# A long convolution and a gated layer on one core: the first batch's last step cut in four parts, some of its matrices made earlier, and work shared out anew in the first steps

## The chip, the cores and the metric

The kernel runs on one core of a Trainium2 chip. A core has five engines that run side by side, each working through its own queue in order: TensorE (PE in the profile; PEld is its weight load), VectorE (DVE), ScalarE (ACT), GpSimd (POOL) and SyncE (SP), which here issues all DMA transfers. They meet through semaphores. The metric is the time of one execution on the device in microseconds (us); of several runs the median counts.

## What is computed

```python
def _attn_ref(x, v, pos_emb, w1, w2):           # x, v: (4, 12480, 128)
    h_mlp = np.maximum(pos_emb @ w1, 0.0) @ w2
    window = np.exp(-0.01 * pos)[:, None]
    h_filt = h_mlp * window                      # a filter as long as the sequence
    u = x * v
    y = irfft(rfft(u, n=2 * S) * rfft(h_filt, n=2 * S))[:, :S, :]
    return x * y                                 # -> 49920 rows of 128

def _moe_ref(x, w_in, w_out):                    # w_in: 128 x 2048, w_out: 2048 x 128
    h = x @ w_in
    g = h * np.cos(h)
    return g @ w_out
```

All is float32; the weights of the gated layer arrive as 64-bit numbers and are converted on the chip.

## The kernel before

**The convolution.** The transform of each batch is written as matrix products over a sequence cut into 120 x 96 places. A batch goes through: the product u = x * v with sums and differences of mirrored rows (30 units, `u_units`, lines 381 to 391); a first forward step (`f1_units`, 64 units: PE L394, then the result is evicted from PSUM, in `f1_evict`, by ACT for even units and by DVE for odd ones, `f1_takers`); a second forward step, which also multiplies with the transformed filter (`f2_units`, 48 units); a first inverse step (`i1_units`, 64 units: PE L457, ACT copies half of the result to `other` at L465, DVE adds and subtracts it at L467), called the third step here; and the last step (`i2_units`, 30 units of four rows each: PE L482 with four matrices `tm`, DVE multiplies by x at L487, SP stores to `zd`). The filter goes through the first two steps as well, before and beside batch 0.

**The matrices of the last step.** A matrix is rows of sines and cosines turned by an angle (`turn`, L271 to L287): ACT multiplies one table (L280), and then DVE multiplies the other and adds in one instruction (L282); or, where a `spare` buffer is given, POOL multiplies (L285) and adds (L287). For batch 0 each unit of `i2_units` makes its four matrices in `before`, three with DVE and one with POOL, all at once and one unit ahead, and SP stores the group to `td`; batches 1 to 3 load their groups from `td`.

**The tables.** `Tables.sines` computes the arguments of a sine table in four or five instructions on one engine (DVE for the forward tables, POOL for the inverse ones) and then has ACT take the sine (L219). The inverse tables are made beside the filter's first step: one sine for each five parts of the step.

**The conversions.** `convert_units` turns the 64-bit weights to float32 in eight pieces, w_in beside batch 0's first step and w_out beside its third, one piece in fourteen parts of the step. A piece has `float32_parts` (DVE two instructions, POOL three, ACT two) and `float32_join` (DVE L151, POOL L156; for w_in a store to memory). The join of a piece stands behind the parts of the next.

**The order of the work.** It is written out by hand: each of these is a generator, and `units` yields after each part with what that part is worth in gate steps. Before batch 0's last step there is no gated layer yet, and the stages follow each other. From then on the main loop walks 98 row tiles x 16 gate steps (`moe_up`, L691 to L700; `moe_act`, L705 and L707; `moe_down`, L716), and after each step takes parts of the convolutions until the step's worth is used up. One unit of batch 0's last step is worth `FIRST_STEPS` = 3.4 gate steps. `inverse_units` takes parts of the next batch's product beside it. The first gate tile can start when two groups of batch 0 have come back from `zd`.

Of the kernel before, what the change touches and what calls it, by code (L numbers as in the profile page):

```python
# [30 lines left out]
def kernel(  # L31
# [135 lines left out]
    def convert_units(pool, pieces):  # L167

        raws, half = [], None
        for i in range(len(pieces) + 1):  # L170
            while len(raws) < min(i + 2, len(pieces)):
                raws.append(pool.tile([P, WCOL, 2], U32, name="raw", bufs=3))
                nc.sync.dma_start(raws[-1][:, :, :], pieces[len(raws) - 1][1])
            yield
            last = half
            if i < len(pieces):
                half = float32_parts(pool, raws[i])
            if i > 0:
                float32_join(pieces[i - 1][0], raws[i - 1], *last)


    class Tables:
        def __init__(self, pool, engine):
            self.pool, self.engine = pool, engine
            self.prod, self.moved = (
                pool.tile([P, P], F32, name=name) for name in ("prod", "moved"))
# [8 lines left out]
        def sines(self, row, column, turn, outs, eighths=None):  # L195


            p, n = outs[0][0].shape
            base = self.prod[0:p, 0:n]
            self.engine.tensor_scalar(out=base, in0=row[0:p, 0:n],  # L200
                                    scalar1=column[0:p, 0:1], scalar2=None, op0=ALU.mult)
            if eighths is not None:
                self.engine.tensor_scalar(out=base[:, eighths], in0=base[:, eighths],
                                        scalar1=float(turn // 8), scalar2=None, op0=ALU.add)
            for dst, quarters in outs:
                turned = self.pool.tile([P, P], F32, name="turned", bufs=2)
                m, t = self.moved[0:p, 0:n], turned[0:p, 0:n]
                if isinstance(quarters, int):
                    quarters = float(quarters * turn // 4)
                self.engine.tensor_scalar(out=m, in0=base, scalar1=quarters,  # L210
                                        scalar2=None, op0=ALU.add)

                self.engine.tensor_scalar(out=t, in0=m, scalar1=1.0 / turn, scalar2=ROUND,
                                        op0=ALU.mult, op1=ALU.add)
                self.engine.tensor_scalar(out=t, in0=t, scalar1=ROUND, scalar2=float(turn),
                                        op0=ALU.subtract, op1=ALU.mult)
                self.engine.tensor_tensor(t, m, t, op=ALU.subtract)
                yield
                nc.scalar.activation(dst, t, AF.Sin, scale=TWO_PI / turn)  # L219

    def forward_tables(pool):
        t = Tables(pool, nc.vector)
# [22 lines left out]
    def inverse_tables(pool):  # L245

        t = Tables(pool, nc.gpsimd)
# [12 lines left out]
                           eighths=slice(H - 1, N2, H))  # L260
        for kept, made in ((csd, cs), (rowsd, rows), (twd, tw_t)):
            nc.sync.dma_start(kept[:, :, :], made[:, :, :])
# [9 lines left out]
    def turn(dst, first, second, one, other, half=None, spare=None):  # L272


        term = dst
        if half is not None:
            term = half()[0:dst.shape[0], 0:math.prod(dst.shape[1:])]
            if len(dst.shape) == 3:
                term = term.rearrange("p (a b) -> p a b", a=dst.shape[1])
        nc.scalar.activation(term, first, AF.Copy, scale=one)  # L280
        if spare is None:
            nc.vector.scalar_tensor_tensor(out=dst, in0=second, scalar=other, in1=term,  # L282
                                           op0=ALU.mult, op1=ALU.add)
        else:
            nc.gpsimd.tensor_scalar(out=spare, in0=second, scalar1=other, scalar2=None,  # L285
                                    op0=ALU.mult)
            nc.gpsimd.tensor_tensor(dst, term, spare, op=ALU.add)  # L287
# [110 lines left out]
    def f1_takers(b):  # L398

        if b % 2 == 0:  # L400
            return nc.scalar.copy, lambda out, in_: nc.scalar.activation(
                out, in_, AF.Copy, scale=-1.0)
# [3 lines left out]
    def f1_evict(ps, b):  # L406
        copy, negated = f1_takers(b)
# [7 lines left out]
    def f1_evict_filter(ps, b):  # L415

        copy, negated = f1_takers(b)
# [82 lines left out]
    def units(n, steps, before, mm, after, parts, ahead=2):  # L500

        for j in range(min(ahead, n)):
            before(j)
        yield 0.0
        last = iter(())
        for j in range(n):
            if j + ahead < n:
                before(j + ahead)
            now = None
            for i in range(parts):  # L510
# [4 lines left out]
                next(last, None)  # L515
                yield steps / parts
            next(last, None)
# [4 lines left out]

    REST = 3.0
    U_STEPS, F1_STEPS, F2_STEPS, I1_STEPS, I2_STEPS = 2.0, 0.8, 2.9, 0.8, 1.5
    FIRST_STEPS, I2U_STEPS = 3.4, 3.0
# [21 lines left out]
    def f1_units(bank, u, evict=f1_evict):  # L547
# [6 lines left out]
        return units(CB, F1_STEPS, lambda j: None, mm, lambda j, ps: evict(ps, j), 2)  # L554
# [57 lines left out]

    def i2_units(bank, b, bufs):

        with tc.tile_pool(name="back", bufs=2) as pool:
            ts, xss = {}, {}

            def before(j):
                ts[j] = pool.tile([N1, G, 2, R], F32, name="tm", bufs=bufs)
                if b == 0:  # L620
                    for i in range(G):
                        if i < G - 1:
                            make_t(ts[j][:, i, :, :], n2s(j)[i])
                        else:
                            spare = pool.tile([N1, 2, R], F32, name="spare", bufs=1)
                            make_t(ts[j][:, i, :, :], n2s(j)[i], spare=spare[:, :, :])
                    nc.sync.dma_start(td[j, :, :, :, :], ts[j][:, :, :, :])
                else:
                    nc.sync.dma_start(ts[j][:, :, :, :], td[j, :, :, :, :])
                xss[j] = pool.tile([R, 2, UA * D], F32, name="xs", bufs=bufs)  # L630
                load_pairs(xss[j], x, b, n2s(j)[0], n2s(j)[UA])

            def mm(j, ps, i):
                if i == 0:
# [5 lines left out]
                             lambda j, ps: i2_out(pool, ps, xss.pop(j), b, j), 2,  # L640
                             ahead=bufs - 1)

    def inverse_units(bank, b):
# [3 lines left out]
        if b + 1 == B:  # L647
            yield from i2_units(bank, b, 3)
            return
        new = u_units(b + 1, 3, slots[0:R, :, :, :], lambda j, half: nc.vector,  # L650
                      side="right")
        for i, steps in enumerate(i2_units(bank, b, 2)):
            if i >= 5:
                for _ in range(1 + i % 2):
# [90 lines left out]
    with tc.manual_schedule():  # L745
        with tc.tile_pool(name="psum", bufs=8, space=PSUM) as psum, \
# [14 lines left out]
            with tc.tile_pool(name="layers", bufs=1, side="right") as pool:  # L761
# [8 lines left out]
                for i in range(1, NCH):  # L770
                    pes[i] = filter_load(pool, i)
                first_u = u_units(0, 3, slots[0:R, :, :, :],
                                  lambda j, half: nc.vector if half and j % 3 else nc.gpsimd)
# [29 lines left out]
            f1 = f1_units(bank, ftile[0:FR, :, :, :], f1_evict_filter)  # L803
# [13 lines left out]
            def beside(units, pieces, bufs):  # L817
                with tc.tile_pool(name="convert", bufs=bufs) as pool:
                    convert = convert_units(pool, pieces)
# [3 lines left out]
                    for _ in convert:  # L823
                        pass

            beside(f1_units(bank, slots[0:R, :, :, :]), [(wind[:, c], w) for c, w in in_pieces], 1)
# [16 lines left out]
            beside(i1_units(bank), [(w_out_sb[:, c, :], w) for c, w in out_pieces], 1)  # L843
# [83 lines left out]
```

## Time and profile before

| what | us |
|---|---|
| median of three runs (3817.17 to 3817.78) | 3817.72 |
| the profiled execution | 3821.13 |
| its span, first to last instruction | 3819.3 |
| PE busy in the span | 3713.3 (97%) |
| DVE busy | 2804.5 (73%) |
| ACT busy | 2488.4 (65%) |
| POOL busy | 2559.8 (67%) |

The profile is that of one execution. "Busy" adds up instructions; an idle engine is shown with what released it ("0.55 <-ACT other L465": idle 0.55 us until ACT's instruction that wrote `other`). A group row gives line, engine, operation, tiles and shapes, count, then busy us and mean ns of one, then idle time before it and its releasers. A row of a stretch gives the busy times of the engines between two points of the span, with the number of instructions in brackets. A line number is a line of the kernel before; helpers such as `turn` and `u_multiply` carry the line for all who call them.

### The profile page before, as it was taken

The page shows a single profiled execution, that of the slowest core. Times are in us where ns is not written, and L with a number is a line of the kernel's source. Part 1 is how long each engine was busy: PE and PEld are TensorE (multiplying, and loading weights), DVE is VectorE, ACT ScalarE, POOL GpSimd, SP SyncE. Part 2 cuts the span into 40 slices and gives each one's busy share as a digit, 9 for nine tenths or more (in the row PEclk, how much of TensorE's full clock was granted, in tenths as well). Part 3 has the DMA queues.
Part 4 walks back from the last instruction along what each step waited for, and adds up shares of the span by engine and source line. Part 5 has one row for each costly group of instructions (what it writes and reads, how often), then busy time and mean ns, then how long its engine had stood idle before and what let it go on. Part 6 is the DMA issues. An engine that isn't in the chain of part 4 may idle for free.

```text
span 3819.3 us, 47226 instructions
## 1 busy us (share of the span) xinstructions
PE 3713.3 (97%) x13546; PEld 2117.3 (55%) x13546; DVE 2804.5 (73%) x5737; ACT 2488.4 (65%) x4597; POOL 2559.8 (67%) x2307
## 2 busy tenths in 40 slices
PE   7797989999999999999999999999999999999999
PEld 6777545655566555545566556555566544444444
DVE  7796898678876787787766787787765566666666
ACT  5654666766665556766655567666664677777777
POOL 6564776478854665588845664788644577777776
PEclk9898999999999999999999999999999999999999
DMA  6163442022201651122203640222105200000000
GB/s 164 49 174 93 134 144 79 12 72 78 77 25 29 188 175 30 31 75 78 68 12 96 182 131 12 57 75 77 49 18 164 83 17 22 18 17 23 17 17 17
DMA packets 209082, 274.65 MB, mean 72 GB/s; under 512 B 17062, under 2 KB 146486, under 8 KB 208694
## 3 DMA queue, kind: packets, MB, share of 16 engines
q1 hardware_dynamic: 208822, 271.63, 24.5%
q8 instruction: 109, 1.79, 0.2%
q14 instruction: 151, 1.24, 0.1%
HBM read 191.93 MB, written 79.63 MB: 71 GB/s over the span
## 4 chain that ended last, share of the span: by engine, by line
PE 85%; DVE 5%; POOL 3%; DMA 3%; ACT 2%; issue 2%; SPq 0%; DVEq 0%; POOLq 0%; ACTq 0%
PE ph L691 32%; PE acc L716 28%; PE cv L716 5%; PE cv L482 5%; PE cv L457 4%; PE cv L394 3%; PE cv L433 3%; PE ph L126 2%; POOL f L700 2%; DMA hd<-h 2%; PE ps L457 1%; ACT cs L705 1%; DVE k L697 1%; PE ps L394 1%; DVE xt L382 1%
## 5 line engine op out<-in xcount | busy, mean ns | idle before, releaser
L700 POOL TENSOR_TENSOR f<-a,k 128x512 f32<-128x512 f32 x1568 | 1989.4, 1269 | 1070.6 <-DVE k L697 1067.8
L691 PE MATMUL ph<-at,w_in_sb 128*128 128x512 f32 x3136 | 1602.7, 592 | 18.6 <-DVE gt L707 18.2
L694 ACT ACTIVATE a<-ph,quarter 128x512 f32<-128x512 f32 x1568 | 1073.3, 684 | 756.9 <-PE ph L691 747.8
L716 PE MATMUL acc<-gt,w_out_sb 128*128 128x512 f32 x2656 | 1362.4, 594 | 5.5 <-ACT ot L722 5.3
L707 DVE TENSOR_TENSOR gt<-ph,cs 128x512 f32<-128x512 f32 x1568 | 1078.1, 688 | 326.4 <-ACT cs L705 298.2
L697 DVE TENSOR_SCALAR k<-a 128x512 f32<-128x512 f32 x1568 | 781.5, 498 | 599.4 <-ACT a L694 583.6
L705 ACT ACTIVATE cs<-f 128x512 f32<-128x512 f32 x1568 | 980.3, 625 | 363.8 <-POOL f L700 362.2
L716 PEld LDWEIGHTS acc<-gt,w_out_sb 128*128 128x128 f32 x2656 | 500.9, 189 | 651.2 <-issue 614.1
L691 PEld LDWEIGHTS ph<-at,w_in_sb 128*128 128x128 f32 x3136 | 553.9, 190 | 358.3 <-issue 262.9
L452 POOL TENSOR_TENSOR slots<-slots,t 120x256 f32<-120x256 f32 x384 | 310.9, 816 | 63.0 <-DVE t L451 25.8
L482 PEld LDWEIGHTS cv<-slots,tm 96*104 96x104 f32 x1920 | 243.0, 172 | 100.0 <-issue 86.0
L482 PE MATMUL cv<-slots,tm 96*104 96x128 f32 x1920 | 254.6, 275 | 3.8 <-DVE tm L282 3.8
L716 PE MATMUL cv<-gt,w_out_sb 128*128 128x512 f32 (+1 forms) x480 | 238.5, 579 | 1.0 <-DVE gt L707 1.0
L457 PEld LDWEIGHTS cv<-cs,slots 120*96 120x96 f32 x1536 | 176.9, 167 | 69.1 <-issue 68.7
L457 PE MATMUL cv<-cs,slots 120*96 120x120 f32 x1536 | 183.2, 266 | 0.0
L433 PE MATMUL cv<-slots,w 124*120 124x256 f32 x576 | 173.0, 380 | 0.0
L433 PEld LDWEIGHTS cv<-slots,w 124*120 124x120 f32 x576 | 103.3, 184 | 122.4 <-issue 109.4
L394 PEld LDWEIGHTS cv<-c,slots 104*124 104x124 f32 x768 | 132.8, 192 | 63.8 <-issue 58.3
L716 PEld LDWEIGHTS cv<-gt,w_out_sb 128*128 128x128 f32 x480 | 90.9, 190 | 110.2 <-issue 106.9
L394 PE MATMUL cv<-c,slots 104*124 104x192 f32 x768 | 150.4, 326 | 0.0
L382 DVE TENSOR_TENSOR xt<-xt,vt 104x256 f32<-104x256 f32 x200 | 143.0, 717 | 0.7 <-DMA vt<-in_v_dram 0.4
L467 DVE TENSOR_TENSOR slots<-cv,other 96x240 f32<-96x240 f32 x384 | 133.6, 394 | 2.8 <-ACT other L465 2.8
(125 smaller groups left out, 2529.3 us busy)
## 6 DMA issues: line engine op xcount, KB each, us to landing
h<-hd SPq DMA_DIRECT2D x144, 240.0 KB
tm<-td SPq DMA_DIRECT2D x90, 312.0 KB
xt<-in_x_dram SPq DMA_DIRECT2D x120, 208.0 KB
vt<-in_v_dram SPq DMA_DIRECT2D x120, 208.0 KB
xs<-in_x_dram SPq DMA_DIRECT2D x120, 208.0 KB
zd<-zs SPq DMA_DIRECT2D x120, 208.0 KB
zb<-zd SPq DMA_DIRECT2D x97, 256.0 KB
w<-wd SPq DMA_DIRECT2D x144, 116.2 KB
```

The lines of the kernel that those rows point to most:

```text
L394: nc.tensor.matmul(ps[0:KE, i * 2 * N1:(i + 1) * 2 * N1], u[:, b, 0:KE, i], c1[0:u.shape[0], :, :].rearrange("p r k -> p (r k)"), start=Tr ...
L433: nc.tensor.matmul(pi, w[:, i, :], parts[0:KE, :, k], start=True, stop=True)
L452: nc.gpsimd.tensor_tensor(y[:, r], y[:, r], t[:, r], op=op)
L457: nc.tensor.matmul(ps[0:N1, (i * 2 + r) * N2:(i * 2 + r + 1) * N2], parts[0:N2, r, :, b, i], cs[:, r, :], start=True, stop=True)
L482: nc.tensor.matmul(ps[0:R, i * D:(i + 1) * D], t[:, i, r, :], slots[0:N1, :, place, :], start=(r == 0), stop=(r == 1))
L691: nc.tensor.matmul(ph[:, 0:m], w_in_sb[:, c * P:(c + 1) * P], ats[n][:, 0:m], start=True, stop=True)
L694: nc.scalar.activation(a[:, 0:m], ph[:, 0:m], AF.Identity, bias=quarter[:, 0:1], scale=INV_TWO_PI)
L697: nc.vector.tensor_scalar(out=k[:, 0:m], in0=a[:, 0:m], scalar1=ROUND, scalar2=ROUND, op0=ALU.add, op1=ALU.subtract)
L700: nc.gpsimd.tensor_tensor(f[:, 0:m], a[:, 0:m], k[:, 0:m], op=ALU.subtract)
L705: nc.scalar.activation(cs[:, 0:m], f[:, 0:m], AF.Sin, scale=TWO_PI)
L707: nc.vector.tensor_tensor(gt[:, 0:m], ph[:, 0:m], cs[:, 0:m], op=ALU.mult)
L716: nc.tensor.matmul(accs[n][:, 0:m], w_out_sb[:, c, :], gt[:, 0:m], start=(c == 0), stop=(c == NFC - 1))
```

## The change

1. `turn`: where a `spare` is given, its multiply goes from POOL to ACT; POOL keeps the addition.
2. `make_group`: the four matrices of a group are made one at a time, with a yield after each. In batch 0's last step two of four go by DVE and two by ACT and POOL.
3. `SOME`: groups 4, 9, 14, 19, 24 and 29 are made beside batch 0's third step instead, all four matrices by ACT and POOL, and stored; batch 0 loads them like the other batches.
4. `units` takes a generator from `before` and advances it by one with each part; batch 0's last step has four parts a unit instead of two, and is worth 3.5 gate steps a unit.
5. Batch 1's product: in every second unit POOL multiplies the first half. Batch 0's product: from unit 18 on POOL multiplies both halves.
6. `f1_takers` gives ACT 53% of the filter's units (33 of 64) and 55% of batch 0's (35 of 64).
7. `Tables`: for the inverse tables the sine on ACT is issued one table later, with three buffers instead of two.
8. `convert_units`: the join of a piece stands ahead of the parts of the next.

```diff
@@ convert_units
-            last = half
+            if i > 0:
+                float32_join(pieces[i - 1][0], raws[i - 1], *half)
             if i < len(pieces):
                 half = float32_parts(pool, raws[i])
-            if i > 0:
-                float32_join(pieces[i - 1][0], raws[i - 1], *last)
@@ Tables.sines (lag 1 for the forward tables, 2 for the inverse ones)
-                turned = self.pool.tile([P, P], F32, name="turned", bufs=2)
+                turned = self.pool.tile([P, P], F32, name="turned", bufs=self.lag + 1)
...
+                self.waiting.append((dst, t, TWO_PI / turn))
                 yield
-                nc.scalar.activation(dst, t, AF.Sin, scale=TWO_PI / turn)
+                if len(self.waiting) == self.lag:
+                    self.finish(1)
@@ turn
         else:
-            nc.gpsimd.tensor_scalar(out=spare, in0=second, scalar1=other, scalar2=None,
-                                    op0=ALU.mult)
+            nc.scalar.activation(spare, second, AF.Copy, scale=other)
             nc.gpsimd.tensor_tensor(dst, term, spare, op=ALU.add)
@@ f1_takers
-        if b % 2 == 0:
+        if int((b + 1) * share) > int(b * share):
@@ units
-            if j + ahead < n:
-                before(j + ahead)
+            early = iter(before(j + ahead) or () if j + ahead < n else ())
             now = None
             for i in range(parts):
...
                 next(last, None)
+                next(early, None)
                 yield steps / parts
+            for _ in early:
+                pass
@@
-    FIRST_STEPS, I2U_STEPS = 3.4, 3.0
+    SOME = range(4, NG, 5)
+    FIRST_STEPS, I2U_STEPS = 3.5, 3.0
@@ new
+    def make_group(pool, g, t, summed, bufs=1):
+        for i, n2 in enumerate(n2s(g)):
+            if i < G - summed:
+                make_t(t[:, i, :, :], n2)
+            else:
+                spare = pool.tile([N1, 2, R], F32, name="spare", bufs=bufs)
+                make_t(t[:, i, :, :], n2, spare=spare[:, :, :])
+            yield
+        nc.sync.dma_start(td[g, :, :, :, :], t[:, :, :, :])
+
+    def some_groups(pool):
+        for g in SOME:
+            t = pool.tile([N1, G, 2, R], F32, name="some", bufs=2)
+            yield from make_group(pool, g, t, G, bufs=2)
@@ i2_units
-                if b == 0:
-                    for i in range(G):
...
-                    nc.sync.dma_start(td[j, :, :, :, :], ts[j][:, :, :, :])
-                else:
-                    nc.sync.dma_start(ts[j][:, :, :, :], td[j, :, :, :, :])
                 xss[j] = pool.tile([R, 2, UA * D], F32, name="xs", bufs=bufs)
                 load_pairs(xss[j], x, b, n2s(j)[0], n2s(j)[UA])
+                if b == 0 and j not in SOME:
+                    return make_group(pool, j, ts[j], G // 2)
+                nc.sync.dma_start(ts[j][:, :, :, :], td[j, :, :, :, :])
...
-                             lambda j, ps: i2_out(pool, ps, xss.pop(j), b, j), 2,
-                             ahead=bufs - 1)
+                             lambda j, ps: i2_out(pool, ps, xss.pop(j), b, j),
+                             4 if b == 0 else 2, ahead=bufs - 1)
@@ inverse_units
-        new = u_units(b + 1, 3, slots[0:R, :, :, :], lambda j, half: nc.vector,
+        new = u_units(b + 1, 3, slots[0:R, :, :, :],
+                      lambda j, half: nc.gpsimd if b == 0 and j % 2 > half else nc.vector,
                       side="right")
+        parts = 4 if b == 0 else 2
         for i, steps in enumerate(i2_units(bank, b, 2)):
-            if i >= 5:
-                for _ in range(1 + i % 2):
+            if i > 2 * parts:
+                for _ in range(i % parts > 0 if b == 0 else 1 + i % 2):
                     next(new, None)
@@ batch 0's product
-                                  lambda j, half: nc.vector if half and j % 3 else nc.gpsimd)
+                                  lambda j, half: nc.vector if half and j % 3 and j < 18
+                                  else nc.gpsimd)
@@ beside
                         if i % 14 == 0:
                             next(convert, None)
+                        elif i % 5 == 0:
+                            next(other, None)
...
-            beside(i1_units(bank), [(w_out_sb[:, c, :], w) for c, w in out_pieces], 1)
+            beside(i1_units(bank), [(w_out_sb[:, c, :], w) for c, w in out_pieces], some_groups)
```

## The prediction

> **What bounds the kernel now.** I read the busy table of the whole span first, then the same table by stretches, then the groups and the order of time inside the stretches in which TensorE (PE) is not full.
>
> ```profile
> span 3819.3 us, 47226 instructions
> ...
> 63.30:124.40 61.10, 52.66 (x256) 49.05 (x256) 51.44 (x176) 37.76 (x165) 43.55 (x81) 0.83 0.30 85
> 124.40:180.30 55.90, 44.67 (x258) 43.16 (x256) 47.87 (x127) 41.09 (x123) 28.59 (x32) 0.96 0.19 56
> 180.30:289.00 108.70, 97.24 (x481) 74.33 (x481) 92.57 (x288) 53.28 (x139) 67.58 (x96) 0.97 0.57 166
> 289.00:348.40 59.40, 56.00 (x512) 55.51 (x512) 49.14 (x154) 28.12 (x84) 30.09 (x36) 0.95 0.17 55
> 348.40:384.00 35.60, 19.67 (x97) 16.59 (x98) 15.72 (x33) 12.76 (x30) 14.05 (x17) 0.67 0.56 163
> 384.00:640.00 256.00, 233.93 (x840) 125.34 (x839) 229.33 (x381) 159.57 (x311) 189.69 (x176) 0.97 0.44 129
> ```
>
> Columns: stretch, length, busy of PE, PE's weight loads, DVE, ACT, POOL; then PE's granted clock, DMA share, GB/s. The rows are the filter's first step, the first batch's first step, its second, its third, the start-up of the gate, and the first batch's last step beside the gate with batch 1's product. After 700 us every stretch but the drain has PE at 98 to 100%, and the change leaves PE's work alone. So time can only come from before 640 us, and what is saved there is saved at the end.
>
> How much room has the last row? From 3000 to 3200 us PE is full with 113 gate steps and 56 transpose records: 1.707 us a step if a record costs 0.125. From 1200 to 1400 it is full with 84 steps, 400 L482 records, 40 of L457 and 44 transposes; that leaves 0.118 a record, 1.88 us a unit. The row holds 98.5 steps (168), 401 records (47) and 44 transposes (5.5): 220.7 of 256 us. **Room: 35 us.** What keeps PE there:
>
> ```profile
> L700 POOL TENSOR_TENSOR f<-a,k 128x512 f32<-128x512 f32 x98 | 125.4, 1279 | 62.6 <-DVE k L697 61.1 <-PE acc L716 1.4
> L707 DVE TENSOR_TENSOR gt<-ph,cs 128x512 f32<-128x512 f32 x99 | 68.1, 688 | 18.6 <-ACT cs L705 16.1 <-PE cv L482 0.4
> L697 DVE TENSOR_SCALAR k<-a 128x512 f32<-128x512 f32 x98 | 63.0, 643 | 7.0 <-ACT a L694 6.9
> L282 DVE SCALAR_TENSOR_TENSOR tm<-rows,tw_t,tm 96x208 f32<-96x208 f32 x72 | 36.3, 554 | 1.4 <-ACT tm L280 1.3
> L382 DVE TENSOR_TENSOR xt<-xt,vt 104x256 f32<-104x256 f32 x57 | 36.1, 637 | 0.0
> L388 DVE TENSOR_TENSOR slots<-xt 104x256 f32<-104x256 f32 x29 | 27.4, 944 | 0.0
> ```
>
> DVE is 90% busy, and POOL waits 61 us for DVE's k. But k takes 0.41 us where POOL is idle and 0.643 here; the product L382 0.41 against 0.637, the difference L388 0.43 against 0.944, the matrix L282 0.418 against 0.554. Times the counts that is 23+13+15+10 = **some 60 us in which DVE stands behind POOL**. gt, which reads PSUM, does not stretch.
>
> **The last step, 384 to 640.** By the program's order this stretch makes groups 6 to 29 now, and 19 of these after (9, 14, 19, 24, 29 are loaded), with two DVE matrices a group instead of three: 72 to 38 L282, -34 x 0.554 = -18.8 us of DVE. Every second unit's first half of batch 1's product goes to POOL: -14 x 0.637 = -8.9. DVE: 229.3 - 27.7 = 201.6. POOL loses 24 multiplies of 0.917 (-22.0), gains 14 additions of 0.788 (+11.0) and 14 products of 0.83 (L382 on POOL, filter stretch; +11.6): unchanged. ACT gains 18 x 0.455 = 8 us, to 168 of 256. At DVE's share of now (0.896) the stretch would take 225 us: **-31**.
>
> Against this speaks the Trainium skill: "Perfetto Trace Analysis", Optimizing Scalar/DVE Operations, says of GPSIMD and DVE that they share an SBUF port, "so offloading operations between those two might not help"; "SBUF — State Buffer", SBUF: two separate sides, calls it an exclusive lock. The rows agree for k, L382 and L388. By the rule POOL's work and these three share one door. Now, at undisturbed durations: f 98 x 1.27, L388 29 x 0.73, L285 24 x 0.80, L287 24 x 0.62, clearing 0.5 = 180; k 98 x 0.41, L382 57 x 0.41, L388 29 x 0.43 = 76; together 256 of 256 us, full. After: POOL 180 - 19.2 + 8.7 + 10.1 = 180, DVE 76 - 5.7 = 70: 250, **-6**. The rule is not strict to the last: from 800 to 1000 us f 96 x 1.27, L452 66 x 0.73 and k 96 x 0.41 make 209.5 in 200 us with PE full, 4.7% more than fits. 250 / 1.047 = 239: **I take -17**, between -6 and -33 (the room). Four parts a unit help this: now four matrices stand in one burst in front of the gate (1.5 us of ACT, 1.4 to 1.8 of DVE). Spacing of 3.5 instead of 3.4 steps moves gate steps forward out of the full stretch, and is nothing by itself.
>
> DMAs: a fifth of the stores moves to the third step (DMA share 17%); six loads of 312 KB come instead, at a share of 44%. In SP's queue outputs and batch 1's loads stand behind them; but SP now waits 85.7 us for L282's matrices in the same place, so 0.
>
> **Filter's first step.** 63 to 124 us ends with POOL: products until 100.0, then the sine chain until 123.0, and ACT stops in front of it with the banks of its half:
>
> ```profile
> 103.27 0.26 ACT L219 ACTIVATE cs<-turned 120x61 f32<-120x61 f32 x1 [10.99 <-POOL turned L217]
> ```
>
> Sine results one step later (a lag of 2) let ACT evict 2.5 units' share before it stops, but POOL's 23 us stay. What moves them: eight products leave DVE (3.4 us), POOL gains 8 x 0.83 = 6.6 and loses its 11.3 us of waits for DVE's product; one unit of 1.56 us goes from DVE to ACT. POOL starts the sines some 3.5 us earlier: **-3.5**, between 0 and -5 (all DVE work removed).
>
> **First batch's first step.** DVE pays 1.23 us a unit (start to start) x 32 = 39.4, 8 conversions x 1.23 = 9.8, and waits 6.3 for the store of an earlier piece:
>
> ```profile
> 147.39 0.29 DVE L133 TENSOR_SCALAR power<-raw 128x256 uint32<-128x256 uint32 x1 [2.29 <-DMA wind<-power]
> ```
>
> Sum 55.5 of 55.9. After: 29 units (35.7) + 9.8; the join now stands in front of POOL's three operations (1.08+1.08+0.73), so the store leaves 2.9 us earlier and the wait (2.3 at most) goes. ACT: 35 x 1.06 + 6.7 = 44, plus waits for the later sig of 0.65 each: 49. ACT is late next; PE's floor is 41 (97 records in the stretch's first 15.6 us, of 256): **-7**, between -5 and -10.
>
> **Third step.** Here the same swap costs. ACT stops for DVE's sig, and only then copies `other`, for which DVE stops:
>
> ```profile
> 323.04 0.42 ACT L144 ACTIVATE sig<-sig 128x256 f32<-128x256 uint32 x1 [1.29 <-DVE sig L141]
> ...
> 324.06 4.49 DVE L467 TENSOR_TENSOR slots<-ps,other 96x240 f32<-96x240 f32 x14 [0.55 <-ACT other L465]
> ```
>
> With the join's 0.64 us ahead of sig, DVE's wait is 1.1 to 1.2 instead of 0.55: 8 x 0.6 = +4.8. On top come 24 matrices, one in 2.5 units: two ACTIVATEs of 0.385 (start to start), 18.5 us in all, and a POOL addition of 0.62. ACT has two `other` buffers ahead of DVE, 1.26 us of cover for 0.77, so these hide except beside a conversion; if the cover is gone they cost 18.5. POOL: 30 + 15 of 59. **+5**, between +1 and +23.
>
> **Start-up.** Group 4 is loaded and not made, batch 1's second pair of loads (2 x 208 KB) is no longer ahead of the first output's way through memory (5.8 us out, 3.7 us back, PE waiting 12.95): **-1.5**, -4 to +1. At the end one more gate tile uses the single accumulator bank, as the convolutions end three steps later: 37.8/52 = **+0.7**.
>
> Sum: -17 - 3.5 - 7 + 5 - 1.5 + 0.7 = -23.3. The profiled run took 3821.1 (span 3819.3 and 1.8 around it): 3797.8. The three runs' median is 3.4 lower, so **3794.5**, 3785 to 3803 as this case's own range.
>
> **Rivals.** (1) The door decides strictly, the last step gives -6: -12.3, **3805.4**. For it: 256 of 256. Against: 209.5 in 200. (2) The bursts and DVE's load were all that mattered; PE is full from 384: -33 there, -39.3, **3778.4**. For it: from 1200 to 1400 PE is full with products on DVE and loaded matrices. Against: that stretch makes no matrices. (3) Slower: POOL's new products stop for loads. They stand in POOL's queue ahead of f, and f of every step waits. DVE's products waited 2.67 and 2.66 us for v at 406 and 543 us. Fifteen stops of 2.66 are +39.9: **3834**; it is slower from 2.06 us a stop. Against: in this stretch DVE stops so only twice, and loads are asked for a unit ahead. (4) The third step's cover is gone: +18.5 more, -4.8, 3813: no difference. That the change doesn't do what it says is excluded by the instruction counts (L282's tm 90 to 48, POOL's L382 40 to 63).
>
> **Numbers.** Forecast 0.50, rival 1 0.22, rival 2 0.14, rival 3 0.06, rival 4 0.08. About 0.2% (7.6 us) is what can be told from no change. Faster 0.86, same 0.08, slower 0.06. Range 3774 to 3810: it takes in rivals 1 and 2.
>
> **What would show it.** First batch's first step near 49 us without waits for the store; sines starting near 96; third step near 64, with longer waits of L467 for `other`; in the last step DVE near 85%, POOL above 80%, k still above 0.6 us. It is wrong if POOL's L382 shows DMA waits, or if the last step gains under 6 or over 30.

## The result, and the profile after

The changed kernel takes **3798.46 us** in the median of four runs (3796.12 to 3799.64) against 3817.75 (3817.17 to 3819.08) of the kernel before beside it; the ratio is 0.9948 (95% interval 0.9931 to 0.9965). The forecast was 3794.5 in a range of 3774 to 3810. The profiled execution took 3799.64, its span is 3797.9 us. The table by stretches of the changed kernel, cut at the same points of the program as that of before (length; busy of PE, weight loads, DVE, ACT, POOL; PE's clock, DMA share, GB/s):

```profile
63.60:117.00 53.40, 48.20 (x256) 46.04 (x257) 48.82 (x163) 37.13 (x163) 46.55 (x85) 0.89 0.33 96
117.00:168.10 51.10, 45.42 (x258) 44.19 (x256) 42.74 (x118) 43.10 (x130) 31.42 (x37) 0.93 0.21 65
168.10:275.90 107.80, 96.77 (x481) 74.52 (x481) 93.20 (x288) 55.89 (x149) 67.72 (x96) 0.97 0.57 166
275.90:340.10 64.20, 56.01 (x512) 54.57 (x512) 48.66 (x150) 41.70 (x129) 44.23 (x58) 0.96 0.25 76
340.10:373.20 33.10, 19.71 (x90) 16.41 (x91) 12.57 (x25) 14.06 (x33) 10.68 (x14) 0.67 0.58 164
373.20:629.20 256.00, 243.56 (x896) 133.00 (x895) 217.39 (x353) 184.00 (x353) 217.47 (x191) 0.99 0.45 134
```

In the last row PE has 243.6 busy us of 256 instead of 233.9, DVE fewer, ACT and POOL more. To compare kernels whose stages start at different times I use one set of marks in every trace: a stage runs from its first PE record to that of the next (the third step to its last one), the start-up from there to the first `gt`, the last step from the first `gt` to the thirtieth `zs`. In the kernels that share the changed kernel's last step it took 226.6 to 229.4 us: differences under 3 us in that row say nothing.

| stage, us | before | after | difference | forecast |
|---|---|---|---|---|
| filter's and first batch's first step together | 119.0 | 106.5 | -12.5 | -10.5 |
| second step | 106.6 | 105.7 | -0.9 | 0 |
| third step | 55.8 | 60.5 | +4.7 | +5 |
| start-up of the gate | 32.9 | 30.4 | -2.5 | -1.5 |
| last step (90 gate steps done by its end, then 93) | 239.9 | 229.4 | -10.5 | |
| from there to the end | 3201.7 | 3201.7 | 0 | |

With the 0.3 us by which the first row starts later this makes the -21.4 of the span. The last two rows belong together. Three gate steps more lie in the last step, 3 x 1.707 = 5.1 us: for equal work it gained 10.5 + 5.1 = **15.6** (forecast 17). What follows has three steps fewer and should be 5.1 us shorter, but is not: **5 us are lost after 600 us** (forecast 0.7).

The groups of the last step, changed kernel, 373.2 to 629.2 us:

```profile
L725 POOL TENSOR_TENSOR f<-a,k 128x512 f32<-128x512 f32 x106 | 134.4, 1268 | 39.7 <-DVE k L722 38.6 <-DMA out_dram<-ob 1.1
L732 DVE TENSOR_TENSOR gt<-ph,cs 128x512 f32<-128x512 f32 x106 | 72.7, 686 | 13.1 <-ACT cs L730 10.6 <-PE ph L716 0.3
L722 DVE TENSOR_SCALAR k<-a 128x512 f32<-128x512 f32 x107 | 57.7, 540 | 26.8 <-ACT a L719 25.4 <-POOL tm L295 1.3
L295 POOL TENSOR_TENSOR tm<-tm,spare 96x208 f32<-96x208 f32 x40 | 43.2, 1079 | 0.0
L291 DVE SCALAR_TENSOR_TENSOR tm<-rows,tw_t,tm 96x208 f32<-96x208 f32 x39 | 37.8, 969 | 0.1
L390 DVE TENSOR_TENSOR xt<-xt,vt 104x256 f32<-104x256 f32 x43 | 33.5, 802 | 0.0
L396 DVE TENSOR_TENSOR slots<-xt 104x256 f32<-104x256 f32 x29 | 15.5, 534 | 0.8 <-POOL xt L390 0.6
L390 POOL TENSOR_TENSOR xt<-xt,vt 104x256 f32<-104x256 f32 x15 | 16.2, 1081 | 0.0
```

Read the means, not only the sums. The matrix on DVE (L291, L282 before) takes 0.969 us instead of 0.554, and POOL's addition (L295, L287 before) 1.079 instead of 0.788. There are 39 such matrices instead of 72, yet together they take 37.8 us instead of 36.3: not one microsecond of DVE's 18.8 came free there. k fell from 0.643 to 0.540 and DVE's difference (L396) from 0.944 to 0.534; that is where DVE's load went down. POOL waits 38.6 us for k instead of 61.1. Nothing in front of POOL's L390 is a DMA.

What reaches PE are its waits for gt. The first row is of the kernel before (384 to 640 us), the second of the changed one (a line number is one of its own kernel):

```profile
L691 PE MATMUL ph<-at,w_in_sb 128*128 128x512 f32 x198 | 106.0, 617 | 15.6 <-DVE gt L707 15.4
L716 PE MATMUL ph<-at,w_in_sb 128*128 128x512 f32 x214 | 110.7, 598 | 5.5 <-DVE gt L732 5.5
```

Between the marks of the last step PE's idle time fell from 22.6 to 12.4 us: 10.2 of the 15.6. The other 5.4 are PE's own busy time for equal work. A gate matmul's record took 0.615 us before and 0.604 after in the mean, at a granted clock of 0.96 and 0.98; no run changes the clock alone, so whether it rose because PE stops less is not shown.

### The profile page after: what moved, and what is told of

Its sections match the earlier page's. It is cut to its first block, busy times and chain, and to the rows that moved or that the text cites. A ratio compares the mean times of both kernels' runs of the same rounds, so it can differ in the third digit from the quotient of the medians.

```text
span 3797.9 us, 47234 instructions
## 1 busy us (share of the span) xinstructions
PE 3706.6 (98%) x13546; PEld 2113.8 (56%) x13546; DVE 2782.8 (73%) x5658; ACT 2520.8 (66%) x4683; POOL 2582.0 (68%) x2342
## 4 chain that ended last, share of the span: by engine, by line
PE 81%; POOL 7%; DVE 4%; ACT 3%; DMA 2%; issue 2%; SPq 0%; POOLq 0%; ACTq 0%; DVEq 0%
PE ph L716 31%; PE acc L741 27%; PE cv L741 5%; PE cv L491 5%; POOL f L725 4%; PE cv L466 4%; PE cv L402 3%; PE cv L442 3%; PE ph L126 2%; DMA hd<-h 1%; DVE k L722 1%; PE ps L402 1%; ACT cs L730 1%; POOL tm L295 1%; PE ps L466 1%
## 5 line engine op out<-in xcount | busy, mean ns | idle before, releaser
L741 PE MATMUL acc<-gt,w_out_sb 128*128 128x512 f32 x2688 | 1376.8, 594 | 9.4 <-ACT ot L747 9.1
L722 DVE TENSOR_SCALAR k<-a 128x512 f32<-128x512 f32 x1568 | 765.2, 488 | 612.1 <-ACT a L719 593.6
L741 PE MATMUL cv<-gt,w_out_sb 128*128 128x512 f32 (+1 forms) x448 | 222.2, 578 | 1.0 <-DVE gt L732 1.0
L390 DVE TENSOR_TENSOR xt<-xt,vt 104x256 f32<-104x256 f32 x177 | 137.3, 783 | 0.0
```

Source lines behind the costliest of these rows:

```text
L722: nc.vector.tensor_scalar(out=k[:, 0:m], in0=a[:, 0:m], scalar1=ROUND, scalar2=ROUND, op0=ALU.add, op1=ALU.subtract)
L741: nc.tensor.matmul(accs[n][:, 0:m], w_out_sb[:, c, :], gt[:, 0:m], start=(c == 0), stop=(c == NFC - 1))
```

## The experiments

All kernels are the changed kernel with the edit shown, and run beside the kernel before. Their order here is by question. Differences of 3 us between two of them lie within their intervals; where I go by stages instead, they are those of one profiled execution each.

### The last step: what made it faster

**All of batch 1's product on DVE**

```diff
-                      lambda j, half: nc.gpsimd if b == 0 and j % 2 > half else nc.vector,
+                      lambda j, half: nc.vector,
```

> The changed kernel with one part undone: batch 1's product on DVE alone. Theory of the shared door (POOL and DVE's SBUF-only instructions take turns; their undisturbed times fit a stretch up to some 1.05 of it): 15 products leave POOL (0.72 each) and come to DVE (0.41), the sum falls by 4.7 us, so the last step gets some 4 us shorter, 3794. Theory of DVE's load (what counts is DVE's busy time, at 0.9 of the stretch): 15 x 0.8 more for DVE, the last step 12 us longer, 3810. If only the spreading of the matrices mattered: no change, 3798.

3798.66 us, ratio 0.9945 (0.9928 to 0.9962); last step 227.0. No difference that can be told: the products POOL took over brought and cost under 3 us.

**Four matrices at once, at the unit's start**

```diff
-                    return make_group(pool, j, ts[j], G // 2)
+                    for _ in make_group(pool, j, ts[j], G // 2):
+                        pass
+                    return
```

> The changed kernel with a group's four matrices made at once at the unit's start, as before, all else kept (four parts, two matrices of four by DVE). Theory of the door and of DVE's load: the same work, at most 3 us longer, 3798 to 3801. Rival (the bursts in front of the gate were the loss): most of the last step's 16 us come back, 3808 to 3814.

3822.13 us, ratio 1.0006 (0.9998 to 1.0015): the whole gain is gone. The last step takes 246.1, the start-up 35.6. The groups of its last step (384 to 630 us):

```profile
L727 POOL TENSOR_TENSOR f<-a,k 128x512 f32<-128x512 f32 x95 | 120.5, 1269 | 48.5 <-DVE k L724 46.6 <-PE ph L126 0.4 <-PE acc L743 0.4
L724 DVE TENSOR_SCALAR k<-a 128x512 f32<-128x512 f32 x94 | 71.4, 759 | 25.0 <-ACT a L721 24.9
L295 POOL TENSOR_TENSOR tm<-tm,spare 96x208 f32<-96x208 f32 x38 | 28.1, 739 | 22.2 <-ACT spare L294 21.5 <-DMA vt<-in_v_dram 0.5
```

POOL's addition stands waiting for ACT's `spare` for 21.5 us, and f of the gate is queued behind it. In the changed kernel's row of L295 that wait is 0.0. With the multiply on ACT a burst has a hand-over in it (ACT, POOL, ACT again for the one `spare` buffer) that it did not have while POOL did both; ACT in turn waits 11.5 us for POOL here, 6.3 in the changed kernel. That the hand-over is what costs is read from these rows and not tried: no run gave the burst a second `spare`, and k is longer here too (0.759 us instead of 0.540).

**Spreading alone**: the last step as before, with one matrix in each of four parts.

```diff
-            nc.scalar.activation(spare, second, AF.Copy, scale=other)
+            nc.gpsimd.tensor_scalar(out=spare, in0=second, scalar1=other, scalar2=None,
+                                    op0=ALU.mult)
...
-    SOME = range(4, NG, 5)
-    FIRST_STEPS, I2U_STEPS = 3.5, 3.0
+    SOME = range(0)
+    FIRST_STEPS, I2U_STEPS = 3.4, 3.0
...
-                    return make_group(pool, j, ts[j], G // 2)
+                    return make_group(pool, j, ts[j], 1)
...
-                      lambda j, half: nc.gpsimd if b == 0 and j % 2 > half else nc.vector,
+                      lambda j, half: nc.vector,
```

> The changed kernel with its first steps, but the last step as before in everything except the spreading: three matrices of a group by DVE and one by POOL with POOL's own multiply, batch 1's product on DVE, no group made early, 3.4 gate steps a unit; only the four parts with one matrix in each are new. Theory of the burst (formed after the four matrices at once gave 3822): the spreading alone is most of the last step's gain, so total 3796 to 3803 (the third step without matrices is back at 56). Theory of the door and of DVE's load: DVE has its 72 L282 and 57 products again and the door's sum is again 256, so the last step is 15 us longer than the changed one's; less 4.5 in the third step: 3808 to 3811.

3819.85 us, ratio 0.9999 (0.9991 to 1.0008). The first steps keep their gain (105.5 us together); the last step takes 245.5 with 90 gate steps, 5.6 more than before, and what follows takes 7.6 more (3209.3). Spreading alone gains nothing, and the new sharing without spreading gains nothing. Its groups, 384 to 630 us:

```profile
L291 DVE SCALAR_TENSOR_TENSOR tm<-rows,tw_t,tm 96x208 f32<-96x208 f32 x69 | 79.2, 1147 | 0.6 <-ACT tm L289 0.3
L294 POOL TENSOR_SCALAR spare<-rows,tw_t 96x208 f32<-96x208 f32 x23 | 27.3, 1185 | 0.0
```

A matrix on DVE takes 1.147 us here, against 0.554 in the bursts of before.

**Three matrices by DVE, one by POOL**, spread, multiply on ACT.

```diff
-                    return make_group(pool, j, ts[j], G // 2)
+                    return make_group(pool, j, ts[j], 1)
```

> The changed kernel, but three of a group's four matrices are made by ACT and DVE and one by ACT and POOL, as in the kernel before; spread over four parts and with the fourth's multiply on ACT, as in the changed kernel. Spreading with the old sharing gained nothing (last step 245.5). Theory A, the number of DVE's matrices decides (19 more L291 of about 1 us, DVE 93% busy instead of 85%): the last step loses 10 to 16 us, time 3809 to 3815. Theory B, POOL's multiply, gone to ACT, is what made the spread pay (POOL loses 19 additions besides): the last step stays within 3 us of the changed kernel's 229, time 3796 to 3802.

3795.65 us, ratio 0.9937 (0.9923 to 0.9952); last step 223.8. **Twenty more matrices on DVE, and the step is not longer but 3 to 6 us shorter** (against 226.6 to 229.4). The stretch from 384 to 630 us and its groups:

```profile
384.00:630.00 246.00, 235.01 (x866) 128.44 (x864) 217.36 (x363) 170.49 (x323) 181.80 (x166) 0.99 0.45 133
```

```profile
L291 DVE SCALAR_TENSOR_TENSOR tm<-rows,tw_t,tm 96x208 f32<-96x208 f32 x56 | 51.7, 923 | 0.7 <-ACT tm L289 0.6
L390 DVE TENSOR_TENSOR xt<-xt,vt 104x256 f32<-104x256 f32 x42 | 24.7, 593 | 0.0
L295 POOL TENSOR_TENSOR tm<-tm,spare 96x208 f32<-96x208 f32 x19 | 15.1, 797 | 0.0
```

DVE is busy for 217.4 of 246 us, 8.5 more than the changed kernel in the same stretch (208.9); POOL for 181.8, 27.3 less. So DVE's busy time does not set the step's length.

**POOL multiplies again**, two and two, spread.

```diff
-            nc.scalar.activation(spare, second, AF.Copy, scale=other)
+            nc.gpsimd.tensor_scalar(out=spare, in0=second, scalar1=other, scalar2=None,
+                                    op0=ALU.mult)
```

> The changed kernel, but the second product of the two matrices made without DVE is taken on POOL again instead of ACT. Theory A (the number of DVE's matrices decides): DVE's work is unchanged, the last step stays within 4 us of 229, time 3798 to 3803. Theory B (POOL's multiply decides): 38 multiplies of 0.92 to 1.19 us more on POOL, 209 + 35 to 45 us of 246, POOL is full: the last step loses 12 to 25 us, time 3811 to 3824.

3843.22 us, ratio 1.0063 (1.0048 to 1.0078): slower than before the change. The last step takes 262.4, 33 us more than with the multiply on ACT, the start-up 36.9 and the third step 63.6. Its groups, 384 to 630 us:

```profile
L291 DVE SCALAR_TENSOR_TENSOR tm<-rows,tw_t,tm 96x208 f32<-96x208 f32 x39 | 50.3, 1291 | 0.2
L294 POOL TENSOR_SCALAR spare<-rows,tw_t 96x208 f32<-96x208 f32 x40 | 50.2, 1255 | 0.0
L492 PE MATMUL cv<-slots,tm 96*104 96x128 f32 x394 | 58.7, 287 | 16.1 <-POOL tm L296 15.5 <-DMA tm<-td 0.6
```

DVE makes as many matrices as in the changed kernel, but each takes 1.291 us, each of POOL's multiplies 1.255, and PE itself waits for the matrix that POOL finishes last. Together with the run before this shows that within the spread form **the multiply that left POOL made the gain, and the matrices that left DVE did not.** Not all of the 33 us is what the change saved: between the marks lie 40 multiplies here, and 25 in the kernel before.

**One sum for all of them.** The forecast's door held POOL's work and k, product and difference of DVE, but left DVE's matrix out. Put it in, at undisturbed durations (POOL: f 1.27, difference 0.73, product 0.83, addition 0.62, multiply 0.80; DVE: k 0.41, product 0.41, difference 0.43, matrix 0.418), times the records between the two marks of the last step. The product's 0.83 is from the filter's stretch; the forecast's door reckoned it at 0.72, which moves the ratios below by 0.01 at most:

| kernel | sum W, us | last step T, us | W / T |
|---|---|---|---|
| before | 267.8 | 239.9 | 1.12 |
| changed | 254.3 | 229.4 | 1.11 |
| product on DVE | 248.8 | 227.0 | 1.10 |
| no groups made earlier (below) | 265.3 | 232.2 | 1.14 |
| spreading alone | 270.5 | 245.5 | 1.10 |
| three and one | 250.2 | 223.8 | 1.12 |
| POOL multiplies | 286.3 | 262.4 | 1.09 |
| four at once | 254.3 | 246.1 | 1.03 |

T goes from 224 to 262 and the ratio stays between 1.09 and 1.14, but for the burst; without the matrix it would go from 0.97 to 1.05 and no longer put the kernels in their order. This sum was made after all the runs, so it describes them and was not tested ahead. PE is also busy for 214 to 233 us of each T, so the sum orders the kernels and is not shown to be their limit. Two limits would fit all rows: the shared work of POOL and DVE, which lets about 1.1 us of undisturbed work through in 1 us, and the hand-over in a burst. Read so, the door would have been the limit before, and bursts cost nothing on top; the new sharing makes the door's work less, and with its hand-over a burst then decides. That would be why each half of the change alone gained nothing.

### The first steps

**The join behind the parts again**

```diff
-            if i > 0:
-                float32_join(pieces[i - 1][0], raws[i - 1], *half)
+            last = half
             if i < len(pieces):
                 half = float32_parts(pool, raws[i])
+            if i > 0:
+                float32_join(pieces[i - 1][0], raws[i - 1], *last)
```

> The changed kernel with the join again behind the parts of the next piece. Theory of the prediction: the third step goes from 60.6 back to about 56 us (DVE's waits for other behind a conversion from 1.1 to 0.55), the first batch's first step, to the first record of the second step, from 53.1 to about 57 with waits of DVE for the store of a piece; total within 2 us of 3798. Rival (the 24 matrices are what lengthens the third step): the third step stays at 60 and the total is 3802.

3807.0 us, ratio 0.9966 (0.9953 to 0.9979). The first batch's first step takes 62.2 instead of 53.1, the third 57.9 instead of 60.5. What DVE waits for in the first of these (120.4 to 182 us; total, times, longest):

```profile
DVE power L133 <- DMA wind<-power: 8.2, 6, 1.8
```

The wait for the store is back; the changed kernel has no such row. Net, the swap is worth 6.5 us by these stages.

**The old split of batch 0's product**

```diff
-                                  lambda j, half: nc.vector if half and j % 3 and j < 18
+                                  lambda j, half: nc.vector if half and j % 3
                                   else nc.gpsimd)
```

> The changed kernel with batch 0's product from unit 18 on shared between DVE and POOL as before. Theory of the prediction: POOL reaches its sines some 3.5 us later (100.5 instead of 97.1), and the filter's first step ends 3.5 later: 57 us instead of 53.4, total 3801 to 3802. Rival (since the lag the sines no longer hold the step): 0 to 1 us.

3801.48 us, ratio 0.995 (0.9935 to 0.9965). POOL's sines start at 99.1 instead of 97.1 us, and both first steps together take 108.8 instead of 106.5.

**The sine one table later: undone**

```diff
-        t = Tables(pool, nc.gpsimd, 2)
+        t = Tables(pool, nc.gpsimd, 1)
...
-        t.finish(1)
```

> The changed kernel with each inverse sine issued on ACT at once, as before (a lag of one). New theory: the lag is what lets the filter's first step end before POOL's sines do (116.9 against 118.9 us), so without it the step ends 4 us later, with ACT's waits for turned again some 10 us: 3802. Theory of the prediction (POOL's chain sets the end in either case): no change, 3798.

3799.7 us, ratio 0.9945 (0.993 to 0.996). The filter's step takes 57.6 instead of 53.4, but the next 48.2 instead of 53.1: 105.8 together against 106.5. The lag moves the boundary between the two and gains nothing.

**Half of the banks for ACT in both steps**

```diff
-            f1 = f1_units(bank, ftile[0:FR, :, :, :], 0.53, f1_evict_filter)
+            f1 = f1_units(bank, ftile[0:FR, :, :, :], 0.5, f1_evict_filter)
...
-            beside(f1_units(bank, slots[0:R, :, :, :], 0.55),
+            beside(f1_units(bank, slots[0:R, :, :, :], 0.5),
```

> The changed kernel with ACT and DVE taking every second unit in the first steps (32 of 64 each). Theory of the prediction: DVE has one unit more in the filter's (+1.5 us, since DVE's work sets its pace) and three more in the first batch's (+3 to +4, 53.1 to 56.5): total 3802 to 3803. Rival (the join's place is all that helped the first batch's first step): no change there, 3798 to 3799.

3804.64 us, ratio 0.9959 (0.9945 to 0.9974). Together 109.7: in the profiles the shares are worth 3.2 us.

### The third step

**No groups made earlier**

```diff
-    SOME = range(4, NG, 5)
+    SOME = range(0)
```

> The changed kernel with no group made beside the third step; all 30 are made in the last step. Theory of the prediction: the third step stays near 60, since the matrices hide there; the last step has five more groups, 10 additions and 10 DVE matrices more: door +6, or DVE's load +10; total 3804 to 3808. Rival (the matrices are what lengthens the third step): it falls to 56 and the total is 3799 to 3803.

3798.68 us, ratio 0.9944 (0.9929 to 0.9959). Third step 55.9 instead of 60.5, start-up and last step 1.1 and 2.8 longer. **Making a fifth of the matrices earlier brought nothing in all**: what it saves later it costs here.

It also undoes the forecast's split of the +5. With the swap and no matrices the step takes 55.9, as before (55.8); with the matrices and the old join 57.9; with both 60.5. So the swap alone is free, and the matrices alone cost 2.1. (In the other kernels with this third step unchanged and the multiply on ACT it takes 60.1 to 60.7.) Waits of the changed kernel in the step (275.9 to 336.4 us), and a conversion in order of time:

```profile
DVE slots L476 <- ACT other L474: 14.2, 23, 1.7
ACT sig L144 <- DVE sig L141: 12.8, 8, 2.0
POOL some L295 <- ACT spare L294: 9.9, 9, 3.5
```

```profile
313.24 0.42 ACT L144 ACTIVATE sig<-sig 128x256 f32<-128x256 uint32 x1 [1.92 <-DVE sig L141]
...
314.26 1.98 DVE L476 TENSOR_TENSOR slots<-ps,other 96x240 f32<-96x240 f32 x6 [1.11 <-ACT other L474]
```

ACT stops 1.92 us for sig, and DVE then 1.11 for `other`, the 1.1 that the forecast gave. But DVE's stops are not what counts. Without the early groups they are there as well (277 to 333 us of that run), 1.1 us each; what is new in the changed kernel is that PE waits for DVE:

```profile
DVE slots L476 <- ACT other L474: 11.7, 11, 1.5
```

```profile
PE ps L466 <- DVE slots L476: 4.5, 5, 1.3
```

PE waits 4.5 us for DVE's slots in the changed kernel, 1.7 with the old join, 0.4 without the early groups and not at all before: nearly what the step is longer by (4.7, 2.1, 0.1, 0). A theory: without the matrices ACT makes a stop for sig good before the next; with two ACTIVATEs for a matrix in every 2.5 units it has less slack to do so. The next run takes the stop away and leaves the matrices.

**A conversion in two lots, nine parts apart**: DVE's sig and power first; ACT's two, POOL's three and the join later.

```diff
...
             yield
+            if i < len(pieces):
+                bits = float32_parts(pool, raws[i])
+            yield
             if i > 0:
                 float32_join(pieces[i - 1][0], raws[i - 1], *half)
             if i < len(pieces):
-                half = float32_parts(pool, raws[i])
+                half = float32_sum(pool, raws[i], *bits)
...
-                        if i % 14 == 0:
+                        if i % 14 in (0, 9):
                             next(convert, None)
-                        elif i % 5 == 0:
+                        if i % 5 == 0 and i % 14:
```

> The changed kernel, but each conversion's instructions are put down in two lots, nine parts apart, in both steps that convert: first DVE's two (power and sig), then ACT's two, POOL's three and the join. The same instructions, none added. Theory: the third step's 4.6 us come from the swap and the matrices together, because ACT stops for DVE's sig (12.8 us in all) and DVE then stops for ACT's other (14.2 us). With sig long there, ACT doesn't stop: third step 60.5 to about 56, first batch's first step unchanged or 1 to 2 better; the span 4 to 6 us shorter, about 3793. Rival: it is ACT's work for the matrices alone (two ACTIVATEs in 2.5 units) that DVE waits for: third step stays at 59 to 61, the time within 2 us of the changed kernel.

3796.26 us, ratio 0.9939 (0.9922 to 0.9955). The third step takes 55.6, as the theory had it, with the matrices in it. Its conversion in order of time:

```profile
312.39 0.28 DVE L141 TENSOR_SCALAR sig<-raw 128x256 uint32<-128x256 uint32 x1
...
313.36 0.42 ACT L148 ACTIVATE sig<-sig 128x256 f32<-128x256 uint32 x1
...
314.49 1.97 DVE L483 TENSOR_TENSOR slots<-ps,other 96x240 f32<-96x240 f32 x6
```

No bracket behind ACT's or DVE's: neither stops, DVE's wait for `other` in the step fell from 14.2 to 6.9 us, and PE never waits for DVE's slots. So neither the stops for sig nor ACT's work for the matrices costs anything alone; together they made the 4.7. The start-up behind it takes 27.0 instead of 30.4, which the expectation did not name. The expectation missed for the first batch's first step: 57.2 instead of 53.1, since a later join means a later store, and DVE waits for it again (4.7 us in five stops). Much of the gain was given back there.

### Three edits together

The lots nine parts apart in the third step alone, three and one in the last step, and one thing found in the trace of later batches: with a share of 0.5 the new `f1_takers` gives the odd units to ACT, where `b % 2 == 0` had given it the even ones.

```diff
...
-        if int((b + 1) * share) > int(b * share):
+        if b % 2 == 0 if share == 0.5 else int((b + 1) * share) > int(b * share):
...
-                    return make_group(pool, j, ts[j], G // 2)
+                    return make_group(pool, j, ts[j], 1)
...
-                        if i % 14 == 0:
+                        if i % 14 == 0 or apart and i % 14 == 9:
```

> The changed kernel with three edits, each of which acts in a stretch of its own. (1) Conversions in two lots, in the third step alone, since in the first batch's first step the later join brought the store waits back. (2) Three matrices by DVE and one by POOL, spread. (3) In the first steps of batches 1 to 3 the even units' banks go to ACT again, as in the kernel before; the change had turned them round without saying so, since the sum of shares of 0.5 passes a whole number at the odd ones. Theory: (1) third step 55.6 instead of 60.5, first batch's first step still 53; (2) last step 224 to 227 instead of 229.4; (3) the waits of PE for DVE's evictions about 36 us after the end of each batch (1.1, 1.6 and 1.6 us) go, and what follows the last step's end takes 3197 to 3198 instead of 3201.7. Together 3784 to 3788. Rival to (3): the order in which a unit's loads are asked for, or the later start of the gate, costs the 5 us: what follows stays at 3201 to 3202, together 3788 to 3792.

**3788.01 us** (3784.16 to 3789.55), ratio 0.9911 (0.9895 to 0.9928), below both kernels; the interval lies under that of the changed kernel (0.9931 to 0.9965). Third step 54.5, start-up 25.5 (30.4 in the changed kernel), last step 223.1 with W / T = 1.12, first batch's first step 53.3. The third edit missed: PE still stops for an eviction 35 us after the end of batch 0's last step (1.20 us; in the next two batches 0.9 each instead of 1.4), and from the last step to the end it took 3202.9 instead of the 3197 to 3198 expected. Which units ACT takes is not what the 5 us are lost to.

## Why the prediction was right, and where its steps were not

**The sign, the size and the place were right.** Time comes from before 640 us, the last step gives most of it when counted for equal work (15.6, the first steps 12.5), and what is saved there stays saved, but for the 5 us above.

**Last step, -17: measured -15.6, by other terms than the sum named.** "DVE: 229.3 - 27.7 = 201.6", with 18.8 of it from matrices, was wrong: three and one has 20 of these matrices back and is shorter. The door was the better sum with the wrong content: with the matrix in it, it orders the kernels. The size of -17 was partly luck. Only 6 of it was work taken from the door; the other 11 came from dividing the work after by 1.047 and that before by 1, and the corrected sum gives both kernels the same ratio (1.12 and 1.11). The Trainium skill, "SBUF — State Buffer", SBUF: two separate sides, counts DVE instructions with two SBUF inputs among those that contend with POOL, and L291 is one: the text of the rule would have included it, and the forecast's stretched 0.554 beside 0.418 said so too. Its "exclusive lock" is not borne out to the letter, as by this sum 1.09 to 1.14 us of undisturbed work go through in 1 us. By the corrected sum the terms are: 25 multiplies gone (-20.0), 15 additions more (+9.3), 35 matrices gone (-14.6), 13 products from DVE to POOL (13 x 0.42 = +5.5), and, as three more gate steps lie in the stage, four more f and three more k (+6.3): -13.5, and divided by 1.11 some -12, where -10.5 was measured. (Undoing the products alone shortened the step by 2.4 us, which is within the noise.)

"Four parts a unit help this" was far too weak: without them the gain is nil. Of the signs named, DVE's 85% (217.4 of 256) and POOL's 85% came; k "still above 0.6 us" did not (0.540).

**Filter's first step -3.5 and first batch's -7: -12.5 together.** The boundary between them moves with the sine's lag, so only the sum can be read. The forecast had the store wait right (it is gone; it reckoned 6.3 us of waits, and undoing the swap costs 9.1 there) and the eight products (2.3 measured of the 3.5). It gave the shares 1.56 us of DVE's work in the first and 3.7 in the second; they measure 3.2 together. PE's granted clock in the filter's step rose from 0.83 to 0.89, but with the lag undone it was 0.89 too and the step 57.6 us, so the clock does not order these steps. Sines start at 97.1 us, where 96 was said; the stretch of the first batch's first step is 51.1 us long, where 49 was.

**Third step +5: +4.7, by luck.** The forecast charged the swap with 4.8 and let the matrices hide; the runs show that the swap alone costs nothing and the matrices 2.1, and only both together 4.7. The step that failed is "8 x 0.6 = +4.8": the wait grew as said (0.55 to 1.11), but DVE's wait is not PE's: without the early groups DVE waits 11.7 us for `other` and PE 0.4 for DVE.

**Start-up -1.5: -2.5.** It was not taken apart. It grew by 5.2 us in the burst, fell by 3.4 with the conversions in two lots, by 1.3 with three and one and by 4.9 with the three edits, so it hangs on how the first matrices are made and on the conversions ahead of it, which the forecast's two transfers left out.

**End +0.7: 5 us.** Behind the thirtieth `zs` PE is idle for 15.9 us instead of 12.5: three stops for DVE's evictions in later batches' first steps are new (3.8 us), two for loads are gone (5.4), and shorter ones for ACT's `ot` and for DVE's gt grew. PE's own busy time fell by 3.2 us there, where three steps fewer should make 5.1. Turning the evictions back did not help, and the order in which later batches' loads are asked for, also changed, was not tried: the cause stays open. Spreading alone loses still more (7.6 us), without those stops for evictions, so neither they nor the sharing of the last step can be the whole of it.

**The rivals.** The strict door (-6) and bursts and DVE's load (-33) frame what came. Of the second, the bursts did matter, since without spreading nothing is gained, and DVE's load did not. In the changed kernel no product stopped for a load. The third step's cover was not gone: +18.5 would have shown.

## What to carry to other kernels

Before moving work off a busy engine, ask whether its instructions are long in themselves or stretched by a neighbour: a sum of undisturbed durations over all who share the path, made afterwards, puts these kernels in order to within some 3 us (the burst apart); the busy time of DVE does not. Move work to an engine outside that sharing (here ACT), and when the hand-over then crosses engines, spread it, since in the burst here the engines waited for each other in front of the gate. Two edits can each be worth nothing alone and all of it together, so undo both one at a time and do each one alone.

## What the hardware showed that was not expected

The same DVE instruction on 96 x 208 took 0.498 us in bursts beside ACT's multiply, 0.969 spread, 1.147 spread beside some multiplies of POOL and 1.291 beside more of them. POOL's multiply and DVE's matrix were both longer side by side (1.255 and 1.291, where each alone was 0.80 and 0.418), while f on POOL stayed at 1.27 in nearly every kernel (1.315 with spreading alone) and it was the instruction beside it that took longer. L151, the join, moved ahead of POOL's operations, took 0.42 us where it had taken 0.64 behind them.
